# Eight row tiles normed one by one, six of them on GpSimd, and a last output unit in two banks with plain stores

## The chip, the cores and the metric

One core of a Trainium2 chip runs the whole kernel. Its engines work side by side, each through its own list in order: TensorE (PE; its weight loads are PEld), VectorE (DVE), ScalarE (ACT), GpSimd (POOL) and SyncE (SP), which issues most of the DMAs. They wait for one another by semaphores. The metric is device time in microseconds (us) of one execution, the median of several runs.

## The reference

The input x (called q) has 2048 rows of 1024. It is normed by rows, and two branches and x itself are summed:

```python
xn = _layernorm(x, axis=-1)                 # (x - mean) / sqrt(var + 1e-5)
return x + _A_ref(xn, k, v, shift_k, ssm_k, ssm_D) + _B_ref(xn, w1, w2)
# _A_ref: q * (long causal convolution of (short convolution of k) * v, by FFT over 4096 points)
# _B_ref: silu(xn @ w1) @ w2        w1: 1024 x 3584, w2: 3584 x 1024
```

## The kernel before

All matrix products run on TensorE in float16. Each operand is split into a high and a low float16 part, and three products stand for one in float32 (lines 979 to 984 and 1111 to 1117). The split of a factor is one instruction on ScalarE for the high part and one on VectorE for the low part (`split`, line 370). The first product of the feed-forward (x by w1) runs over pairs of 128 columns of w1; most pairs are computed in units of seven products of half-size blocks (`units`), the first two pairs directly (`plain_unit`). The second product (by w2) runs the same way, ends with eight such units of seven products (`units2`), and the last of these ends the kernel. The convolution's transforms run between these units on VectorE, ScalarE and TensorE.

The order is set by a planner (`Order.run`, line 167). Each stream of work is a generator that yields operations with an assumed duration; the planner takes the one that could start earliest, less the bias of its stream, and writes it down on its engine. What was written down is the program, and no engine changes its order later. While the constant stream is set (`order.spare`), the planner fills assumed gaps of TensorE with matmuls of constants that nothing reads.

The start goes like this. SyncE loads the 16 row tiles `xt` (128 rows by 1024 each) and the blocks of w1 (`x` and `raw`). For a tile VectorE takes two `bn_stats` and a `bn_aggr` (mean and variance into `stat`), GpSimd raises variance + 1e-5 to the power -0.5 (`rstd`), and the tile is normed in place (subtract the mean, multiply by `rstd`). Tiles 0 and 1 are treated alone, 2 and 3 together, 4 to 7 together, 8 to 15 together (`ln_rows`, line 528). Tiles 3, 5 and 7 are normed on ScalarE, with `nmr` = -mean * `rstd` as bias; the other five of the first eight on VectorE. TensorE transposes a normed tile in two halves into banks `ft` (three banks in turn; a fourth, `nm`, takes the small sums of squares of w1), and ScalarE and VectorE split them into the operands `x` (x_215 and x_216 for tiles 0 to 3). The first plain unit works through its rows in parts (tile 0, tile 1, tiles 2 and 3), and for each part through both column blocks j (`wo_190` and `wo_191`).

The last unit of `units2` (u = 7) has three result banks: `c` for P7 and P4, `two` for P6, P5 and P3, `one` for P1 and P2. P4 is added into `c` in two halves of 256 columns, and each half is scaled, summed and stored by a plain DMA from SyncE (line 1242). The other results go out by DMAs from GpSimd's queue that add to what is in memory (`G`).

## Time and profile before

| | us |
|---|---|
| median of 3 runs (lowest to highest) | 1247.47 (1245.33 to 1250.55) |
| the profiled execution | 1249.43 |
| its span, first to last instruction | 1247.7 |
| TensorE busy in it | 1230.0 |
| VectorE, ScalarE, GpSimd busy | 1120.0, 744.7, 142.6 |

TensorE's busy time counts a matmul until its modelled end, so a wait shows a little shorter than it is. A row of a timeline gives start, duration, engine, line, operation, what is written and read, a count where equal instructions are merged, and in brackets the idle time ahead of it with what ended it. Line numbers are those of the kernel before.

### The profile page before, as it was taken

What the parts mean: (1) busy time and instruction counts of PE and PEld (TensorE: products, weight loads), DVE (VectorE), ACT (ScalarE), POOL (GpSimd) and SP (SyncE); (2) the same over time, 40 slices, a digit from 0 to 9 for tenths busy, and PEclk for the clock granted to TensorE, in tenths of its full rate; (3) what the DMA queues carried; (4) which work ended last, traced back from release to release, by engine and by line L of the source; (5) the groups of instructions that cost most, each with busy time, mean ns of one, the idle gap of its engine ahead of it and who ended that gap; (6) DMA issues with size and microseconds to landing.
All of it is one profiled execution on the core that took longest, in us unless ns stands there. A gap on an engine that the chain in (4) does not pass through costs nothing.

```text
span 1247.7 us, 17185 instructions
## 1 busy us (share of the span) xinstructions
PE 1230.0 (99%) x6089; PEld 593.7 (48%) x6089; DVE 1120.0 (90%) x1360; ACT 744.7 (60%) x1303; POOL 142.6 (11%) x155
## 2 busy tenths in 40 slices
PE   8999999999999999999999999999999999999998
PEld 6544544444444444445444444544454454445444
DVE  7999996988799879998999799889979979998992
ACT  7867987878677767758663632563273264526231
POOL 1100000000000020002010300310030030113114
PEclk9999999999999999999999999999999999999999
DMA  9268998989999798969998787699596587978766
GB/s 337 77 223 301 329 311 274 301 277 350 302 357 287 252 260 269 277 213 266 338 293 228 154 264 177 153 250 269 126 214 172 134 169 239 252 157 139 164 144 93
DMA packets 254293, 292.93 MB, mean 235 GB/s; under 512 B 48768, under 2 KB 167808, under 8 KB 252032
## 3 DMA queue, kind: packets, MB, share of 16 engines
q1 hardware_dynamic: 227472, 266.93, 68.2%
q0 software_dynamic: 26736, 24.92, 14.9%
q8 instruction: 47, 0.77, 0.2%
q14 instruction: 38, 0.31, 0.1%
HBM read 193.22 MB, written 98.57 MB: 234 GB/s over the span
## 4 chain that ended last, share of the span: by engine, by line
PE 70%; DVE 18%; DMA 5%; issue 3%; ACT 2%; POOL 0%; SPq 0%; DVEq 0%; ACTq 0%
PE ff L981 10%; PE ff L982 10%; PE ff L983 10%; PE ff L1114 10%; PE ff L1116 10%; PE ff L1115 10%; DVE spec L349 6%; DVE tmp L349 2%; PE ps L1581 2%; PE ps L1583 2%; PE ps L1582 2%; DVE x L352 2%; DVE ht L352 1%; DMA wraw<-in_w 1%; DVE hf L349 1%
## 5 line engine op out<-in xcount | busy, mean ns | idle before, releaser
L1114 PE MATMUL ff<-x,wo 128*128 128x512 f16 x868 | 328.1, 378 | 1.8 <-ACT hf L360 1.2
L1116 PE MATMUL ff<-x,wo 128*128 128x512 f16 x868 | 328.1, 378 | 0.0
L1115 PE MATMUL ff<-x,wo 128*128 128x512 f16 x868 | 328.1, 378 | 0.0
L981 PE MATMUL ff<-x,wo 128*128 128x512 f16 (+2 forms) x824 | 304.1, 371 | 1.6 <-ACT wo L360 1.4
L983 PE MATMUL ff<-x,wo 128*128 128x512 f16 (+2 forms) x824 | 304.1, 371 | 1.5 <-DVE wo L352 1.4
L982 PE MATMUL ff<-x,wo 128*128 128x512 f16 (+2 forms) x824 | 304.1, 371 | 0.7 <-DVE x L352 0.7
L349 DVE TENSOR_TENSOR spec<-spec 128x1024 f32<-128x1024 f32 (+2 forms) x272 | 263.3, 1001 | 2.3
L1114 PEld LDWEIGHTS <-wo 128*128 128x128 f16 x868 | 84.9, 98 | 101.8 <-issue 1.3
L1116 PEld LDWEIGHTS <-wo 128*128 128x128 f16 x868 | 84.9, 98 | 101.6
L1115 PEld LDWEIGHTS <-wo 128*128 128x128 f16 x868 | 84.9, 98 | 101.6 <-issue 2.2
L983 PEld LDWEIGHTS <-wo 128*128 128x128 f16 x824 | 80.6, 98 | 94.7 <-DVE wo L352 1.8
L981 PEld LDWEIGHTS <-wo 128*128 128x128 f16 x824 | 80.6, 98 | 90.1 <-ACT wo L360 1.6
L982 PEld LDWEIGHTS <-wo 128*128 128x128 f16 x824 | 80.5, 98 | 87.3 <-issue 0.5
L346 POOL DMA_DIRECT2D out<-hf x59 | 52.0, 884 | 452.2 <-ACT hf L360 335.9
L360 ACT ACTIVATE hf<-ff,invc 128x512 f32<-128x512 f32 x60 | 40.9, 681 | 100.2 <-PE ff L1116 74.8
L346 POOL DMA_DIRECT2D out<-yt x56 | 62.3, 1300 | 335.1 <-DVE yt L352 195.2
L349 DVE TENSOR_TENSOR tmp<-spec 128x2048 f32<-128x2048 f32 (+1 forms) x48 | 92.6, 1934 | 0.9
L352 DVE SCALAR_TENSOR_TENSOR ht<-hf,wsc,ht 128x1024 f16<-128x1024 f32 (+1 forms) x56 | 67.2, 1203 | 12.8 <-ACT ht L360 12.7
L360 ACT ACTIVATE spec<-spec 128x1024 bf16<-128x1024 f32 x32 | 33.7, 1054 | 62.3 <-DVE spec L349 62.2
L360 ACT ACTIVATE spec<-ps 128x512 f32<-128x512 f32 x96 | 55.5, 591 | 18.8 <-PE ps L1583 17.2
L352 DVE SCALAR_TENSOR_TENSOR wo<-raw,wsc,wo 128x512 f16<-128x512 f32 (+1 forms) x56 | 56.6, 1013 | 10.0 <-ACT wo L360 9.5
L360 ACT ACTIVATE ht<-hf,wsc 128x1024 f16<-128x1024 f32 (+1 forms) x56 | 60.6, 1085 | 4.4 <-DVE hf L349 2.8
(175 smaller groups left out, 1759.8 us busy)
## 6 DMA issues: line engine op xcount, KB each, us to landing
wo<-hs SPq DMA_DIRECT2D x160, 256.0 KB, 3.7
hs<-ht SPq DMA_DIRECT2D x80, 256.0 KB, 4.8
wraw<-in_w SPq DMA_DIRECT2D x31, 512.0 KB, 5.4
out<-hf POOLq DMA_DIRECT2D x59, 256.0 KB, 4.2
raw<-in_w SPq DMA_DIRECT2D x28, 512.0 KB, 6.3
kin<-in_kp SPq DMA_DIRECT2D x16, 704.0 KB, 6.1
kf<-in_fs SPq DMA_DIRECT2D x8, 1024.0 KB, 5.5
hsfS<-ht SPq DMA_DIRECT2D x32, 256.0 KB, 3.8
```

Of the source, the lines that this page charges most:

```text
L346: return Op("POOL", 1.1, 4.8, lambda: nc.gpsimd.dma_start(o, i, accum_op=ADD), [i], [o], m, n)
L349: return V(lambda: nc.vector.tensor_tensor(o, a, b, op=op), o, [a, b], **k)
L352: return V(lambda: nc.vector.scalar_tensor_tensor(o, a, s, b, op0=op0, op1=op1), o, [a, b] + ([] if isinstance(s, float) else [s]), **k)
L360: nc.scalar.activation(o, i, func, scale=scale, **kw)
L981: nc.tensor.matmul(o, w[:, 0, k], xf[:, :, k, 0], start=first and k == 0, stop=False, **kw)
L982: nc.tensor.matmul(o, w[:, 0, k], xf[:, :, k, 1], start=False, stop=False, **kw)
L983: nc.tensor.matmul(o, w[:, 1, k], xf[:, :, k, 0], start=False, stop=last and k == KH - 1, **kw)
L1114: nc.tensor.matmul(o, hx[:, n, 0, :], wc[:, n, 0, q], start=first and n == 0, stop=False, **kw)
L1115: nc.tensor.matmul(o, hx[:, n, 0, :], wc[:, n, 1, q], start=False, stop=False, **kw)
L1116: nc.tensor.matmul(o, hx[:, n, 1, :], wc[:, n, 0, q], start=False, stop=last and n == 3, **kw)
L1581: nc.tensor.matmul(o, cf[:, 0], hi[i], start=i == 0, stop=False, **kw)
L1582: nc.tensor.matmul(o, cf[:, 0], lo[i], start=False, stop=False, **kw)
```

## The change

In the start, `ln_rows` makes a stream for each of tiles 0 to 7 (`norm_rows`), and each tile has its own chain on GpSimd: -mean, variance + 1e-5, the power, `nmr`. Tiles 2 to 7 are normed on GpSimd too; tiles 0 and 1 stay on VectorE, and ScalarE norms none. The scratch tiles `st` and `mv` get six buffers in place of two. The constant matmuls at the very start are 18 in place of 26. The banks `ft` and `nm` become one ring of four, in which late transposes leave one free. In the first plain unit both parts of the first two tiles run for column block 0 before block 1. The planner assumes the first DMAs to land 1 us earlier.

In the last unit, P7 and P4 go to two banks, one for columns 0 to 383 and one for 384 to 511. The tile that P3 ends (`at(u, 0, 1)`) is no longer added to memory from GpSimd's queue: its present value is loaded ahead of time (`o2`), summed on VectorE and stored by a plain DMA.

```diff
@@ -179,7 +179,8 @@
             _, t, s = best
             op, (r, w) = s.head, s.touched
             if self.spare is not None and op.eng == "PE":
-                for _ in range(int((t - self.free["PE"] - 0.1) / 0.22)):
+                op.fills = max(0, int((t - self.free["PE"] - 0.1) / 0.22))
+                for _ in range(op.fills):
...
@@ -191,7 +192,7 @@
             done = t + op.busy
             end = done + op.late
             if op.nbytes:
-                self.pipe = max(self.pipe, t + 3.0) + op.nbytes / 330e3
+                self.pipe = max(self.pipe, t + (2.0 if t < 3.0 else 3.0)) + op.nbytes / 330e3
...
@@ -430,8 +431,7 @@
-    ft = Ring(order, ps_e, "ft", 3)
-    nm = Ring(order, ps_e, "nm", 1)
+    nm = ft = Ring(order, ps_e, "ft", 4)
...
     def ln_rows():
-        for t0, n, bias in ((0, 1, 0.26), (1, 1, 0.26), (2, 2, 0.17), (4, 4, 0.15), (8, 8, 0.03)):
-            yield bias
+        for t in range(8):
+            add(norm_rows(t, 1), (0.26, 0.26, 0.17, 0.17, 0.1, 0.1, 0.1, 0.1)[t])
+        for t in range(8):
+            yield flag["xn", t]
+        yield from norm_rows(8, 8)
+
+    def norm_rows(t0, n):
+            yield flag["xt", t0]
             q = slice(t0, t0 + n)
-            mv = lnp.tile([P, 8], F32, name="mv", bufs=2)
-            m = mv[:, 0:n]
+            mv = lnp.tile([P, 2, 8], F32, name="mv", bufs=6)
+            m, minus = mv[:, 0, 0:n], mv[:, 1, 0:n]
             order_in = (8, 9, 12, 13, 10, 11, 14, 15) if n == 8 else range(t0, t0 + n)
             for t in order_in:
                 yield flag["xt", t]
                 xt = xts[t][0]
-                st = lnp.tile([P, 2, 6], F32, name="st", bufs=2)
+                st = lnp.tile([P, 2, 6], F32, name="st", bufs=6)
                 for a in range(2):
                     yield V(lambda: nc.vector.bn_stats(st[:, a, :], xt[:, a * W:(a + 1) * W]), st[:, a, :],
                             [xt[:, a * W:(a + 1) * W]], us=0.65)
                 yield V(lambda: nc.vector.bn_aggr(stat[:, t, :], st), stat[:, t, :], [st], us=0.2)
 
             def chain(m=m, q=q):
+                if n < 8:
+                    nc.gpsimd.tensor_scalar(minus, stat[:, q, 0], -1.0, None, op0=MUL)
                 nc.gpsimd.tensor_scalar(m, stat[:, q, 1], 1e-5, None, op0=ADD)
                 nc.gpsimd.tensor_tensor(rstd[:, q], m, power, op=ALU.pow)
-                if n in (2, 4):
-                    nc.gpsimd.tensor_scalar(m, stat[:, q, 0], -1.0, None, op0=MUL)
-                    nc.gpsimd.tensor_tensor(nmr[:, q], m, rstd[:, q], op=MUL)
             power = half.to_broadcast([P, n])
-            p = V(chain, rstd[:, q], [stat[:, q, :]], us=1.2)
+            p = V(chain, rstd[:, q], [stat[:, q, :]], us=1.0 + 0.25 * n)
             p.eng = "POOL"
-            p.writes.append(m)
-            if n in (2, 4):
-                p.busy += 0.5
-                p.writes.append(nmr[:, q])
+            p.writes += [m, minus]
             yield p
+            if n < 8:
+                p = V(lambda: nc.gpsimd.tensor_tensor(nmr[:, q], minus, rstd[:, q], op=MUL), nmr[:, q],
+                      [minus, rstd[:, q]], us=0.3)
+                p.eng = "POOL"
+                yield p
             if n == 8:
                 yield V(lambda: nc.vector.scalar_tensor_tensor(nmr, stat[:, :, 0], -1.0, rstd, op0=MUL, op1=MUL),
                         nmr, [stat, rstd])
             for t in order_in:
                 xt = xts[t][0]
-                if t in (3, 5, 7):
+                if t in (2,3,4,5,6,7,):
+                    p = V(lambda: nc.gpsimd.tensor_scalar(xt, xt, stat[:, t, 0:1], rstd[:, t:t + 1], op0=SUB, op1=MUL),
+                          xt, [xt, stat[:, t, :], rstd[:, t:t + 1]], us=1.2)
+                    p.eng = "POOL"
+                    yield p
+                    flag["xn", t].set()
+                    continue
+                if t in ():
                     yield a_act(xt, xt, AF.Identity, rstd[:, t:t + 1], nmr[:, t:t + 1])
                     flag["xn", t].set()
                     continue
...
             yield flag["xn", t]
             xn, tok = xns[t]
-            yield ft.ready
+            yield ft.ready if t < 8 else lambda: len(ft.free()) > 1
             pt, ptok = ft.tile([P, KH, P], uses=2)
...
-        for q, j in [(slice(([0] + list(ends))[n], e), j) for n, e in enumerate(ends) for j in range(2)]:
+        parts_of_rows = [slice(([0] + list(ends))[n], e) for n, e in enumerate(ends)]
+        todo = [(q, j) for q in parts_of_rows for j in range(2)]
+        if len(ends) == 3:
+            todo = [(q, j) for j in range(2) for q in parts_of_rows[:2]] + todo[4:]
+        for q, j in todo:
...
             c = ff.tile([P, W])
-            add(evacuate2(u, one, c, made, seen), EB)
-            yield from product2("P7", u, c[0], True)
+            banks = [c]
+            if last:
+                banks.append(seen["more"])
+            add(evacuate2(u, one, banks, made, seen), EB)
+            for q, bank in zip(columns(u), banks):
+                if bank is not c:
+                    yield ff.ready
+                    bank.what = ff.tile([P, W])
+                    bank = bank.what
+                yield from product2("P7", u, bank[0], True, q=q)
...
             yield seen["P7"]
-            for q in columns(u):
-                yield from product2("P4", u, c[0], q=q)
+            for q, bank in zip(columns(u), banks):
+                yield from product2("P4", u, (c if bank is c else bank.what)[0], q=q)
                 made["P4", q.start].set()
 
     def columns(u):
 
-        m = 2 if u == len(tiles2) - 1 else 1
-        return [slice(a * W // m, (a + 1) * W // m) for a in range(m)]
+        if u < len(tiles2) - 1:
+            return [slice(0, W)]
+        return [slice(0, 384), slice(384, W)]
...
-    def evacuate2(u, one, c, made, seen):
...
@@ -1214,6 +1241,9 @@
             yield hfs.ready
             o, otok = hfs.tile([P, W])
             yield L(o, at(u, 1, 0))
+            yield hfs.ready
+            o2, otok2 = hfs.tile([P, W])
+            yield L(o2, at(u, 0, 1))
...
         seen["P5"].set()
-        yield v_stt(d, c[0], invc2[:, 0:1], d, MUL, ADD)
+        banks = [banks[0]] + [b.what for b in banks[1:]]
+        for q, c in zip(columns(u), banks):
+            yield v_stt(d[:, q], c[0][:, q], invc2[:, 0:1], d[:, q], MUL, ADD)
...
         yield made["P3"]
-        add(copied(two, k2, at(u, 0, 1)), EB)
-        for q in columns(u):
+        if last:
+            yield v_stt(o2, two, invc2[:, 0:1], o2, MUL, ADD)
+            k2.set()
+            yield L(at(u, 0, 1), o2)
+            otok2.set()
+        else:
+            add(copied(two, k2, at(u, 0, 1)), EB)
+        for q, c in zip(columns(u), banks):
             yield made["P4", q.start]
             yield v_stt(a[:, q], c[0][:, q], invc2[:, 0:1], a[:, q], MUL, ADD)
+            c[1].set()
             yield (L if last else G)(at(u, 1, 0)[:, q], a[:, q])
-        c[1].set()
...
         yield flag["spilled"]
-        yield nm.ready
+        yield lambda: len(ft.free()) == 4
...
         pt, tok = ff.tile([P, 4, P])
-        for _ in range(26):
+        for _ in range(18):
             yield T(lambda: nc.tensor.matmul(pt[:, 0, :], ones, ones, start=True, stop=True), pt[:, 0, :], [], 0.3)
```

GpSimd's list at the start before, for tiles 2 and 3 and then 4 to 7 (545 to 549 are the chain's lines; tiles 0 and 1 have the first two of them each):

```order
L545 TENSOR_SCALAR mv<-stat 128x2 [waits DVE_49]
L546 TENSOR_TENSOR rstd<-mv,half 128x2 [waits Pool_49]
L548 TENSOR_SCALAR mv<-stat 128x2 [waits Pool_49]
L549 TENSOR_TENSOR nmr<-mv,rstd 128x2 [waits Pool_49]
L545 TENSOR_SCALAR mv<-stat 128x4 [waits DVE_49]
L546 TENSOR_TENSOR rstd<-mv,half 128x4 [waits Pool_49]
L548 TENSOR_SCALAR mv<-stat 128x4 [waits Pool_49]
L549 TENSOR_TENSOR nmr<-mv,rstd 128x4 [waits Pool_49]
```

And now for tile 2, whose rows return for each of tiles 3 to 7 (L571 is the norm; tiles 0 and 1 have the first four):

```order
L552 TENSOR_SCALAR mv<-stat 128x1 [waits DVE_49]
L553 TENSOR_SCALAR mv<-stat 128x1
L554 TENSOR_TENSOR rstd<-mv,half 128x1 [waits Pool_49]
L561 TENSOR_TENSOR nmr<-mv,rstd 128x1 [waits Pool_49]
L571 TENSOR_SCALAR xt_242<-xt_242,stat,rstd 128x1024 [waits DMAHW0_49]
```

Each tile has four small instructions in place of two to four for a group, and a norm of 128x1024 stands in the same list between a tile's chain and the next one's.

VectorE's list, from the norm of tile 1 (xt_237) on; xt_242 and xt_246 are tiles 2 and 3, `ft_342` and `ft_365` the transposed halves of tile 1:

```order
L567 TENSOR_SCALAR xt_237<-xt_237,stat,rstd 128x1024 [waits Pool_49]
L352 SCALAR_TENSOR_TENSOR wo_190<-x_225,wsc,wo_190 128x512 [waits DMAHW3_49,DMAHW2_49,Activation_49]
L540 BN_STATS st<-xt_242 128x6 [waits DMAHW0_49]
L352 SCALAR_TENSOR_TENSOR wo_190<-x_225,wsc,wo_190 128x512 [waits DMAHW5_49,DMAHW4_49,Activation_49]
L352 SCALAR_TENSOR_TENSOR wo_191<-x_225,wsc,wo_191 128x512 [waits Activation_49]
L540 BN_STATS st<-xt_242 128x6
L542 BN_AGGR stat<-st 128x2 [waits DVE_49]
L540 BN_STATS st<-xt_246 128x6 [waits DMAHW1_49]
L352 SCALAR_TENSOR_TENSOR x_215<-ft_342,x_215 128x4x128 [waits PE_49,Activation_49]
L352 SCALAR_TENSOR_TENSOR x_216<-ft_365,x_216 128x4x128 [waits PE_49,Activation_49]
L540 BN_STATS st<-xt_246 128x6
L352 SCALAR_TENSOR_TENSOR wo_191<-x_225,wsc,wo_191 128x512 [waits Activation_49]
```

And now (xt_249 is tile 3, xt_264 tile 4, `ft_355` and `ft_379` the halves of tile 1):

```order
L581 TENSOR_SCALAR xt_237<-xt_237,stat,rstd 128x1024 [waits Pool_49]
L353 SCALAR_TENSOR_TENSOR wo_190<-x_224,wsc,wo_190 128x512 [waits DMAHW3_49,DMAHW2_49,Activation_49]
L546 BN_STATS st<-xt_242 128x6
L353 SCALAR_TENSOR_TENSOR wo_190<-x_224,wsc,wo_190 128x512 [waits DMAHW5_49,DMAHW4_49,Activation_49]
L548 BN_AGGR stat<-st 128x2 [waits DVE_49]
L546 BN_STATS st<-xt_249 128x6 [waits DMAHW1_49]
L546 BN_STATS st<-xt_249 128x6
L353 SCALAR_TENSOR_TENSOR x_215<-ft_355,x_215 128x4x128 [waits PE_49,Activation_49]
L353 SCALAR_TENSOR_TENSOR x_216<-ft_379,x_216 128x4x128 [waits PE_49,Activation_49]
L548 BN_AGGR stat<-st 128x2 [waits DVE_49]
L546 BN_STATS st<-xt_264 128x6 [waits DMAHW4_49]
L353 SCALAR_TENSOR_TENSOR wo_191<-x_224,wsc,wo_191 128x512 [waits Activation_49]
```

Tile 2's mean and variance come after two low parts of weights in place of three, both parts for `wo_191` stand behind the low parts of tile 1, and tile 3's `bn_stats` ahead of them.

The end of VectorE's list before, from the last output of the convolution on (`hf_196` is the loaded output, `ff_10328` the bank `c`):

```order
L352 SCALAR_TENSOR_TENSOR wo_195<-ps_10292,csc_8745,ht_199 128x512 [waits DMASW3_49,DMASW2_49,DVE_49]
L352 SCALAR_TENSOR_TENSOR hf_197<-ff_10328,invc_156,hf_197 128x512 [waits Activation_49]
L349 TENSOR_TENSOR hf_197<-hf_197,hf_196 128x512 [waits DMAHW6_49]
L352 SCALAR_TENSOR_TENSOR hf_197<-ff_10328,invc_156,hf_197 128x256 [waits DVE_49,PE_49]
L352 SCALAR_TENSOR_TENSOR hf_197<-ff_10328,invc_156,hf_197 128x256 [waits PE_49]
```

And now, from P7's two sums on (`ff_10352` and `ff_10372` are the two banks, `ff_10353` is `two`):

```order
L353 SCALAR_TENSOR_TENSOR hf_197<-ff_10352,invc_156,hf_197 128x384 [waits Activation_49]
L353 SCALAR_TENSOR_TENSOR hf_197<-ff_10372,invc_156,hf_197 128x128 [waits PE_49]
L350 TENSOR_TENSOR hf_197<-hf_197,hf_196 128x512 [waits DMAHW6_49]
L353 SCALAR_TENSOR_TENSOR hf_196<-ff_10353,invc_156,hf_196 128x512 [waits DMAHW7_49,PE_49]
L353 SCALAR_TENSOR_TENSOR hf_197<-ff_10352,invc_156,hf_197 128x384 [waits DVE_49,PE_49]
L353 SCALAR_TENSOR_TENSOR hf_197<-ff_10372,invc_156,hf_197 128x128 [waits PE_49]
```

P4's two sums at the end have 384 and 128 columns in place of twice 256, each with a bank of its own, and the sum for the plain store of `at(u, 0, 1)` is new ahead of them.

SyncE's last DMAs before:

```order
L337 DMA wo_191<-hsfS_71 128x1024 [waits DMAHW4_49,PE_49]
L337 DMA wo_190<-hsfA_72 128x1024 [waits DMAHW5_49,PE_49]
L337 DMA hf_196<-out 128x512 [waits DMAHW6_49,DMASW1_49,DVE_49]
L337 DMA out<-hf_197 128x256 [waits DMAHW7_49,DMAHW6_49,DVE_49]
L337 DMA out<-hf_197 128x256 [waits DMAHW0_49,DVE_49]
```

And now, from the load for the last unit on:

```order
L338 DMA hf_196<-out 128x512 [waits DMAHW6_49,DMASW1_49,DVE_49]
L338 DMA hf_196<-out 128x512 [waits DMASW6_49,DMAHW7_49,DMASW5_49,DMASW3_49]
L338 DMA out<-hf_196 128x512 [waits DMAHW7_49,DMAHW0_49,DVE_49]
L338 DMA out<-hf_197 128x384 [waits DMAHW6_49,DMAHW1_49,DVE_49]
L338 DMA out<-hf_197 128x128 [waits DMAHW2_49,DVE_49]
```

One load and one store of 128x512 are new on SyncE's queue, and the last store has 128 columns in place of 256. GpSimd's last DMA (`out<-wo_190`, of P3) is gone from its list, and with it ScalarE's last copy.

On TensorE 11 wide constant matmuls stand ahead of the first transposes in place of 5, and 16 in place of 15 ahead of those of tile 1; the sums of squares come between the two halves of tile 0. The two filler matmuls in the middle of the program are there in both, and one more has come ahead of the first unit of the lower rows.

1 line of the change is left out of this document (added).

## The prediction

> **What bounds the kernel now.** I read the page's busy line first, then the windows of TensorE over the whole span, then the timelines of its start and the chain at the end. The page says that TensorE is busy nearly throughout:
>
> ```profile
> span 1247.7 us, 17185 instructions
> PE 1230.0 (99%) x6089; PEld 593.7 (48%) x6089; DVE 1120.0 (90%) x1360; ACT 744.7 (60%) x1303; POOL 142.6 (11%) x155
> ```
>
> So 17.7 us are left in which TensorE does nothing. The windows of 25 us (TensorE's busy time and count, granted clock, DMA share, GB/s) show where they lie:
>
> ```profile
> 0.00:25.00 25.00, 21.08 (x200) 1.00 0.94 344
> 25.00:50.00 25.00, 22.36 (x148) 1.00 0.54 161
> 50.00:75.00 25.00, 25.00 (x120) 1.00 0.29 98
> 675.00:700.00 25.00, 21.45 (x101) 0.93 0.50 118
> 1225.00:1247.70 22.70, 17.36 (x92) 1.00 0.73 101
> ```
>
> There are 6.56 in the first 50 us, 3.55 in one stretch in the middle that the diff does not touch, and 5.34 at the end (a part of which is the last store). The change works at the first and the last place, so it can win some five of those ten microseconds, plus what it saves of constants, and no more; what it does in the start is kept only if TensorE stays full behind it. TensorE's timeline of the start:
>
> ```profile
> 1.06 7.96 PE L1844 MATMUL ff<-one 128*128 128x128 f32 x52 [1.06 <-DVE oneb L403]
> 8.86 1.25 PE L1847 MATMUL ff<-oneb 128*128 128x512 bf16 x5
> 9.95 1.04 PE L586 MATMUL ft<-ident,xt 128*128 128x128 f32 x8
> 10.95 3.44 PE L1847 MATMUL ff<-oneb 128*128 128x512 bf16 x15
> 14.26 1.09 PE L586 MATMUL ft<-ident,xt 128*128 128x128 f32 x8
> 15.19 0.22 PE L981 MATMUL ff<-x,wo 128*128 128x128 f16 x1
> 15.24 0.22 PE L982 MATMUL ff<-x,wo 128*128 128x128 f16 x1
> 18.98 0.23 PE L981 MATMUL ff<-x,wo 128*128 128x128 f16 x1 [1.41 <-ACT wo L360]
> 20.68 0.23 PE L983 MATMUL ff<-x,wo 128*128 128x128 f16 x1 [1.41 <-DVE wo L352]
> 26.91 0.66 PE L586 MATMUL ft<-ident,xt 128*128 128x128 f32 x4 [1.43 <-ACT xt L360]
> 29.70 0.27 PE L982 MATMUL ff<-x,wo 128*128 128x256 f16 x1 [0.72 <-DVE x L352]
> ```
>
> The first 15 us hold constants, then come four waits that sum to 4.97: two for split weights, one for a normed tile that ScalarE finishes (L360), one for a low part on VectorE. The windows leave 6.56 - 1.06 - 4.97 = 0.53 for some six small ones. A shown wait is shorter than the true one: fifteen wide constants take 3.44 and five 1.25, so one costs 0.219 and each group ends in a tail of 0.15 that counts as busy. Ten waits are thus 5.5 + 1.5 = 7.0 us.
>
> **The constants.** 26 matmuls in float32 are 52 passes; 18 are 36. The passes at the end of the row are the fast ones: 52 in 7.96 less the slower first ones. The row up to the 45th pass is
>
> ```profile
> 1.06 7.18 PE L1844 MATMUL ff<-one 128*128 128x128 f32 x45 [1.06 <-DVE oneb L403]
> ```
>
> so one costs 0.78/7 = 0.11, and sixteen fewer give back 1.8. Six more wide constants (11 for 5) cost 6 x 0.219 = 1.3. The transposes of tile 0 come at about 9.5 instead of 9.95. VectorE's low parts of tile 0 follow them, and then the norm of tile 1, on which tile 1's transposes at 14.26 hang. In the new order one `bn_stats` stands between, so I keep 0.4 of the 0.5: first real matmul at 14.8, **-0.4**. Bounds: 0 (if tile 1's norm does not move) and -0.5.
>
> **The norms.** GpSimd's, VectorE's and ScalarE's rows for the chains and norms (group of two for tiles 2 and 3; then four):
>
> ```profile
> 0.24 0.10 POOL L1906 MEMSET const-float32-0.0<- 128x1 f32 x1 [0.24 <-issue]
> 1.00 0.29 POOL masks.py:199 TENSOR_SCALAR_AFFINE_SELECT ident<-ident 128x128 f32<-128x128 f32 x1
> 11.03 0.58 POOL L546 TENSOR_TENSOR rstd<-mv,half 128x1 f32<-128x1 f32 x1
> 20.83 0.23 POOL L545 TENSOR_SCALAR mv<-stat 128x2 f32<-128x2 f32 x1 [9.23 <-DVE stat L542]
> 21.95 0.80 POOL L548 TENSOR_SCALAR mv<-stat 128x2 f32<-128x2 f32 x1
> 17.42 0.21 DVE L542 BATCH_NORM_AGGREGATE stat<-st 128x2 f32<-128x12 f32 x1
> 21.90 0.81 DVE L567 TENSOR_SCALAR xt<-xt,stat,rstd 128x1024 f32<-128x1024 f32 x1 [0.36 <-POOL rstd L546]
> 33.38 1.53 DVE L567 TENSOR_SCALAR xt<-xt,stat,rstd 128x1024 f32<-128x1024 f32 x2 [0.94 <-POOL rstd L546]
> 23.06 1.24 ACT L360 ACTIVATE xt<-xt,nmr,rstd 128x1024 f32<-128x1024 f32 x1 [1.01 <-POOL nmr L549]
> 35.00 2.38 ACT L360 ACTIVATE xt<-xt,nmr,rstd 128x1024 f32<-128x1024 f32 x2 [2.79 <-POOL nmr L549]
> ```
>
> Before, tile 2's variance is ready at 17.63, but the chain waits for tile 3 and starts at 20.83; tile 2 is normed at 22.71, tile 3 at 24.30, tiles 4 and 6 at 34.91, 5 and 7 at 37.38. VectorE sheds three norms (3 x 0.8 = 2.4), ScalarE three (3 x 1.24 = 3.7). GpSimd gets 32 small instructions in place of 12, and six norms, all in series.
>
> A tile's chain on GpSimd is 0.23 for the first instruction, 0.1 more for the second like it, 0.58 for the power, 0.23 for `nmr` and some 0.1 between them: 1.2 us. What a norm of 128x1024 costs there no row shows. From below: 0.81, VectorE's time; the select of 128x128 gives nearly the same, if the 0.23 of an instruction of two columns is its fixed part: 0.23 + 8 x 0.06 = 0.7. From above: if only 0.10 of the select is fixed, as much as a memset of one column takes, 0.10 + 8 x 0.19 = 1.6; if none is, 8 x 0.29 = 2.3. Between 0.8 and 1.6, which have a fixed part, I take the middle, 1.2, since no row is nearer, and keep 0.8 and 2.3 as ends.
>
> GpSimd and VectorE also stand in each other's way. L548 takes 0.80 at 21.95 where its like L545 takes 0.23, and it ends within 0.04 of VectorE's norm that started at 21.90. L545 for four tiles does the same beside two low parts of weights (0.62, to 31.87; the first of the two low parts ends at 31.08 + 1.36/2 = 31.76):
>
> ```profile
> 31.25 0.62 POOL L545 TENSOR_SCALAR mv<-stat 128x4 f32<-128x4 f32 x1 [8.23 <-DVE stat L542]
> 31.08 1.36 DVE L352 SCALAR_TENSOR_TENSOR wo<-x,wsc,wo 128x512 f16<-128x512 f32 x2
> ```
>
> So one small instruction of a chain in the way of such a VectorE instruction loses up to 0.7, and a GpSimd norm holds VectorE's low parts of weights for up to 1.2. The Trainium skill (SBUF — State Buffer, Who interferes with whom) says that a VectorE instruction with two SBUF inputs or in a two-port mode and a GpSimd instruction exclude each other for a whole instruction; the 0.80 beside the 0.81 agrees.
>
> With these durations in the new order I get: tile 2's variance after norm 1 (which ends 0.4 earlier), one low part of 0.7, a `bn_stats`, another low part and 0.21, at 15.8; plus chain 1.2 and norm 1.2 and gaps, 18.5 (was 22.7). Tile 3's variance is now behind the two low parts of tile 1, at 18.4; its chain loses 0.6 to a low part; normed 21.6 (24.3). Tiles 4 and 5 follow at 24.8 and 27.8 (34.2 and 36.2, half way through the rows of two). Tiles 6 and 7 lose: their `bn_stats` stand far down VectorE's list behind eight low parts, so 38.2 and 42.4 (34.9 and 37.4).
>
> What TensorE then waits for: 1.3 up to 17.7 (tile 0's 24 matmuls for column block 0 end 24 x 0.055 after 14.8, at 16.1, and tile 1's need its first low part, which VectorE ends at 17.7 behind two `bn_stats` of tile 3; this takes the place of both waits for weights, since column block 1 comes later), 1.0 at 21.7 (tile 3), 0.5 at 23 (a bank of the ring that VectorE frees), 1.3 at 42.5 (tile 7), and 0.8 of small ones: 4.9 in place of 7.0, **-2.1**. One more filler on TensorE, **+0.2**. The DMAs of the start are the same ones in the same order on SyncE; nothing is moved there. The ring of four leaves late transposes one bank fewer; the window from 50 on, with TensorE 25.00 of 25.00 busy, hides that.
>
> How it hangs on the norm's duration: up to 1.3 nothing is lost (tile 3 alone waits). At 1.6 the wait at tile 3 is 0.4 longer, tiles 4, 5 and 7 a bit later: about -2.5 in all for the whole change. At 2.0 five norms in series are 4 us later than at 1.2, most of it hidden except at tiles 3 and 7, and the sum is about -0.5; the break-even lies near 2.0. From there every norm of the series shows: 0.3 more in five of them is 1.5, and VectorE's low parts, held as long, cost about another 1, so at 2.3 it is +2.
>
> **The end.** TensorE's and VectorE's last rows, in one list by time:
>
> ```profile
> 1236.46 0.75 DVE L352 SCALAR_TENSOR_TENSOR hf<-ff,invc,hf 128x512 f32<-128x512 f32 x1 [8.38 <-ACT hf L360]
> 1241.28 0.27 PE L1116 MATMUL ff<-x,wo 128*128 128x256 f16 x1
> 1241.59 0.48 DVE L352 SCALAR_TENSOR_TENSOR hf<-ff,invc,hf 128x256 f32<-128x256 f32 x1 [3.78 <-PE ff L1116]
> 1242.12 0.27 PE L1114 MATMUL ff<-x,wo 128*128 128x256 f16 x1 [0.57 <-DVE hf L352]
> 1242.98 0.48 DVE L352 SCALAR_TENSOR_TENSOR hf<-ff,invc,hf 128x256 f32<-128x256 f32 x1 [0.91 <-PE ff L1116]
> ```
>
> TensorE stops in P4 until VectorE has read the first half, since both halves stand in one bank: the matmul of 1242.12 would have come at 1241.39, 0.11 after the one before it. With two banks this 0.73 is gone. P4 does not get longer by its new columns: 128-column matmuls follow one another by 0.055 (15.19, 15.24), half of 0.11. VectorE's sum of 384 columns, 0.61 between 0.48 and 0.75, lies beside the twelve matmuls of the second bank (12 x 0.055 = 0.66) and just ends in time. The last sum has 128 columns; by the line through 0.75 and 0.48 it takes 0.34, so -0.14. Then the store, and GpSimd's last adding DMAs of the convolution:
>
> ```profile
> 1229.35 2.20 POOL L346 DMA_DIRECT2D out<-wo  x2 [0.30 <-DMA out<-wo]
> hf<-out SPq DMA_DIRECT2D x1, 256.0 KB, 4.0
> out<-hf SPq DMA_DIRECT2D x2, 128.0 KB, 3.4
> ```
>
> The last plain store is half as large, and P3's adding DMA no longer runs beside it, so -0.2 of 3.4 (between 0 and -0.6). Together **-1.1**, bounds -0.5 and -1.5. The added sum of P3 (0.75 on VectorE) lies under the first 384 columns of P4, twelve matmuls of some 0.16 each, 1.9. The added load waits for the convolution's last adding DMAs, issued by GpSimd up to 1231.55; the last starts about 1230.4, and if it takes about as long as the load (4.0) it lands about 1234.5. Another 4.0 for the load is 1238.5, and it is needed when P3 ends, about 1239.7 (P4's 18 matmuls to 1241.39 begin 18 x 0.11 earlier). If that cover of some 1.2 us fails, VectorE's list stops there, P4's sums stand behind it, and each microsecond late is one more in the end.
>
> **The sum.** -0.4 - 2.1 + 0.2 - 1.1 = -3.4 to -3.5. The profiled execution took 1249.43, 1.96 above the median, so it would be 1245.9, and the median **1244.0**.
>
> **The rivals.** (a) GpSimd's norm is short (0.8, the select's row with 0.23 fixed) and the lock costs nothing: tile 3's wait of 1.0, half of tile 7's and the small rest at the bank go, 2.0 in all: 1242.0. (b) It is 1.6, the same row with 0.10 fixed, or twice VectorE's 0.81: -2.0 to -2.5, so 1245.3. The Trainium skill (GPSIMD Engine Reference, Performance versus the Vector engine) has GpSimd about twice as slow in elementwise work, 4497 ns against 2293; by it the estimate would be 1245.3 as well, and no run here shows it yet. (c) The other side: the norm costs 2.3, the whole select scaled. From 2.0 on the norms in series are what TensorE waits for (tiles 3, 4, 5 and 7): +2.1, 1249.6. For it speaks only that nothing is known of the fixed part; against it, that even a memset of one column has 0.10. (d) The start's gain is given back: behind 50 us TensorE waits for nothing, but VectorE is just as full:
>
> ```profile
> 50.00:55.00 5.00, 5.00 (x25) 2.25 (x23) 5.00 (x9) 4.97 (x9) 0.00 (x0) 1.00 0.14 57
> ```
>
> (TensorE, its loads, VectorE, ScalarE, GpSimd, then clock and DMA.) If the operands made there are on the edge, TensorE comes earlier and waits the same; only the end's -1.1 stays: 1246.4. Against it: VectorE sheds 2.4 and ScalarE 3.7 before that.
>
> **The chances.** Main case 0.44, (a) 0.16, (b) 0.14, (c) 0.13, (d) 0.13. The main case's own range is 1242 to 1246, by the bounds of the start, the end and the middle of the norm's. The whole range, 1240.0 to 1249.5, takes in (a) with the largest end gain and most of (c). A measurement of this kernel can tell about 0.5% from no change, 6.2 us here. Faster than 1241.2 asks for (a) and every bound on the good side: 0.12. Slower than 1253.7 asks for a norm of some 3 us or the late load at the end: 0.04. Within: 0.84.
>
> **What would show it.** In the profile after: the norm's row on GpSimd between 1.0 and 1.4; first real matmul at 14.8; normed tiles 2 and 3 at 18.5 and 21.6, 6 and 7 later than before; waits of TensorE at about 17.7, 21.7 and 42.5, in sum 1.5 to 2 less than before in the first 50 us; from 50 to 75 still 25.00 busy; no wait between the halves of P4 and a last sum of about 0.33. A norm over 2 us, a new wait between 50 and 100, or a wait of VectorE for the loaded tile at 1239 would make it wrong.

## The result, and the profile after

| us | before | after |
|---|---|---|
| median (lowest to highest) | 1247.47 (1245.33 to 1250.55) | 1255.77 (1253.95 to 1258.54) |
| profiled execution, and its span | 1249.43, 1247.7 | 1258.54, 1256.8 |
| TensorE busy | 1230.0 | 1234.0 |

The changed kernel is slower by 0.6%: its time over that before is 1.0063, with a 95% interval of 1.0044 to 1.0081. That is 8.3 us by the medians, and 9.1 between the profiled executions; the one after is the slowest of its five.

The page after, the line of busy times:

```profile
PE 1234.0 (98%) x6094; PEld 596.6 (47%) x6094; DVE 1119.0 (89%) x1359; ACT 741.8 (59%) x1299; POOL 167.5 (13%) x180
```

GpSimd is busy 25 us more, for six norms and some small instructions. TensorE's windows after (busy time and count, granted clock, DMA share, GB/s), the first three stretches, the one that answers to 675 to 700 before (the changed kernel is some 9 us later there), and one further on:

```profile
0.00:25.00 25.00, 19.53 (x155) 0.95 0.94 341
25.00:50.00 25.00, 20.30 (x148) 0.84 0.44 134
50.00:75.00 25.00, 22.48 (x113) 1.00 0.22 62
...
684.00:709.00 25.00, 23.78 (x124) 1.00 0.53 147
...
1075.00:1100.00 25.00, 22.06 (x100) 0.96 0.91 233
```

TensorE idles 12.7 us of the first 75, where before it idled 6.6, and it also runs at a lower clock. GpSimd's timeline after says why; here are all rows of tile 2's chain and norm, then the norms of tiles 3 to 7:

```profile
16.22 0.23 POOL L552 TENSOR_SCALAR mv<-stat 128x1 f32<-128x1 f32 x1 [3.71 <-DVE stat L548]
16.51 0.21 POOL L553 TENSOR_SCALAR mv<-stat 128x1 f32<-128x1 f32 x1
16.80 0.57 POOL L554 TENSOR_TENSOR rstd<-mv,half 128x1 f32<-128x1 f32 x1
17.45 0.19 POOL L561 TENSOR_TENSOR nmr<-mv,rstd 128x1 f32<-128x1 f32 x1
17.62 3.81 POOL L571 TENSOR_SCALAR xt<-xt,stat,rstd 128x1024 f32<-128x1024 f32 x1
...
23.10 3.80 POOL L571 TENSOR_SCALAR xt<-xt,stat,rstd 128x1024 f32<-128x1024 f32 x1
...
28.39 3.80 POOL L571 TENSOR_SCALAR xt<-xt,stat,rstd 128x1024 f32<-128x1024 f32 x1
...
34.46 3.80 POOL L571 TENSOR_SCALAR xt<-xt,stat,rstd 128x1024 f32<-128x1024 f32 x1
...
44.92 3.80 POOL L571 TENSOR_SCALAR xt<-xt,stat,rstd 128x1024 f32<-128x1024 f32 x1
...
50.48 3.80 POOL L571 TENSOR_SCALAR xt<-xt,stat,rstd 128x1024 f32<-128x1024 f32 x1
```

A norm takes 3.80, against 0.81 on VectorE and 1.24 on ScalarE, and with its chain a tile takes 5.2 to 6.0 in one list. Tile 2 is done at 21.4 (22.7 before), tile 3 at 26.9 (24.3), tile 4 at 32.2 (34.2), tile 5 at 38.3 (36.2), tile 6 at 48.7 (34.9), tile 7 at 54.3 (37.4). Only tiles 2 and 4 gain. TensorE's timeline shows all its waits of the start:

```profile
17.92 0.22 PE L996 MATMUL ff<-x,wo 128*128 128x128 f16 x1 [1.07 <-DVE x L353]
21.48 1.09 PE L600 MATMUL ft<-ident,xt 128*128 128x128 f32 x8 [2.12 <-POOL xt L571]
26.96 1.12 PE L600 MATMUL ft<-ident,xt 128*128 128x128 f32 x4 [3.18 <-POOL xt L571]
38.31 1.09 PE L600 MATMUL ft<-ident,xt 128*128 128x128 f32 x8 [2.21 <-POOL xt L571]
48.78 1.09 PE L600 MATMUL ft<-ident,xt 128*128 128x128 f32 x8 [0.53 <-POOL xt L571]
54.34 1.09 PE L600 MATMUL ft<-ident,xt 128*128 128x128 f32 x8 [2.52 <-POOL xt L571]
```

Five waits for a GpSimd norm sum to 10.56 us. Behind the first of them, from 22.7 to 32.9 us, the granted clock is halved (all engines by windows of 2 us; the clock is the third figure from the right):

```profile
22.00:24.00 2.00, 1.77 (x21) 1.50 (x19) 0.22 (x1) 1.83 (x4) 1.84 (x4) 0.67 1.03 412
24.00:26.00 2.00, 0.00 (x0) 0.00 (x0) 1.89 (x5) 0.24 (x1) 2.00 (x1) 0.50 1.05 365
...
30.00:32.00 2.00, 2.00 (x21) 2.00 (x20) 2.00 (x5) 2.00 (x6) 2.00 (x1) 0.50 0.31 103
32.00:34.00 2.00, 2.00 (x20) 1.89 (x18) 2.00 (x4) 1.94 (x4) 1.77 (x4) 0.77 0.08 19
```

The order written for TensorE is the same before and after from about 250 us on, up to the last unit, so a landmark in it measures the lag. Four matmuls of zeros stand in both; first before, then after:

```profile
320.33 0.61 PE L332 MATMUL ff<-one,zero 128*128 128x128 f32 x4
```

```profile
329.59 0.61 PE L333 MATMUL ff<-one,zero 128*128 128x128 f32 x4
```

The lag is 9.26 us there. Of it 6.1 are idle time (12.7 less 6.6). The other 3.2 are the same work taking longer, which fits the clock: of the 10.2 us at half TensorE waits 3.2, and in the other 7.0 it does the work of 3.5. The end is 9.1 late. In between the lag falls and rises again: the stretch from 675 lost 3.55 before and the one from 684 loses 1.22 after, but near 1098 after waits longer than before. First after, then before, each time a wait that ScalarE ends:

```profile
1098.77 0.58 PE L1132 MATMUL ff<-x,wo 128*128 128x512 f16 x1 [2.94 <-ACT hf L361]
```

```profile
1091.21 0.38 PE L1114 MATMUL ff<-x,wo 128*128 128x512 f16 x1 [1.20 <-ACT hf L360]
```

Whether that exchange belongs to the change is one of the questions below.

The end came out nearly as read before. VectorE's last two rows after:

```profile
1249.71 0.75 DVE L353 SCALAR_TENSOR_TENSOR hf<-ff,invc,hf 128x512 f32<-128x512 f32 x1 [1.69 <-PE ff L1134]
1251.66 1.02 DVE L353 SCALAR_TENSOR_TENSOR hf<-ff,invc,hf 128x384 f32<-128x384 f32 x2 [1.20 <-PE ff L1134]
```

The sum of P3 waits for TensorE, not for its load; the last two sums follow one another without a gap, and no wait of TensorE within P4 is left.

### The profile page after: what moved, and what is told of

Same layout as the page of the kernel before. It is cut to its first block, busy times and chain, and to the rows that moved or that the text cites. A ratio compares the mean times of both kernels' runs of the same rounds, so it can differ in the third digit from the quotient of the medians.

```text
span 1256.8 us, 17232 instructions
## 1 busy us (share of the span) xinstructions
PE 1234.0 (98%) x6094; PEld 596.6 (47%) x6094; DVE 1119.0 (89%) x1359; ACT 741.8 (59%) x1299; POOL 167.5 (13%) x180
## 4 chain that ended last, share of the span: by engine, by line
PE 72%; DVE 16%; DMA 5%; issue 3%; POOL 3%; ACT 1%; SPq 0%; DVEq 0%; ACTq 0%
PE ff L1132 12%; PE ff L1133 12%; PE ff L1134 12%; PE ff L995 10%; PE ff L996 10%; PE ff L997 10%; DVE spec L350 5%; DVE tmp L350 2%; POOL xt L571 2%; DMA out<-yt 2%; DVE ht L353 2%; PE ps L1619 2%; PE ps L1621 2%; PE ps L1620 2%; DVE x L353 1%
## 5 line engine op out<-in xcount | busy, mean ns | idle before, releaser
L1132 PE MATMUL ff<-x,wo 128*128 128x512 f16 (+2 forms) x872 | 329.6, 378 | 2.9 <-ACT hf L361 2.9
L1133 PE MATMUL ff<-x,wo 128*128 128x512 f16 (+2 forms) x872 | 329.7, 378 | 0.0
L1134 PE MATMUL ff<-x,wo 128*128 128x512 f16 (+2 forms) x872 | 329.4, 378 | 0.0
L996 PE MATMUL ff<-x,wo 128*128 128x512 f16 (+2 forms) x824 | 306.1, 372 | 1.1 <-DVE x L353 1.1
L997 PE MATMUL ff<-x,wo 128*128 128x512 f16 (+2 forms) x824 | 306.1, 372 | 0.0
L995 PE MATMUL ff<-x,wo 128*128 128x512 f16 (+2 forms) x824 | 306.0, 372 | 0.0
```

The source lines that it names most:

```text
L995: nc.tensor.matmul(o, w[:, 0, k], xf[:, :, k, 0], start=first and k == 0, stop=False, **kw)
L996: nc.tensor.matmul(o, w[:, 0, k], xf[:, :, k, 1], start=False, stop=False, **kw)
L997: nc.tensor.matmul(o, w[:, 1, k], xf[:, :, k, 0], start=False, stop=last and k == KH - 1, **kw)
L1132: nc.tensor.matmul(o, hx[:, n, 0, :], wc[:, n, 0, q], start=first and n == 0, stop=False, **kw)
L1133: nc.tensor.matmul(o, hx[:, n, 0, :], wc[:, n, 1, q], start=False, stop=False, **kw)
L1134: nc.tensor.matmul(o, hx[:, n, 1, :], wc[:, n, 0, q], start=False, stop=last and n == 3, **kw)
```

## The experiments

Theory G was at first that GpSimd's norms are the whole loss; rival H that the chains by tile, the ring of four and the order of the blocks cost as well.

### The norms put back, the end alone, the start alone

```diff
-                if t in (2,3,4,5,6,7,):
+                if t in ():
...
-                if t in ():
+                if t in (3, 5, 7):
```

> The changed kernel with one edit: tiles 2, 4 and 6 are normed on VectorE and 3, 5 and 7 on ScalarE, as before the change; the chains by tile, the ring, the order of the blocks and the end stay. Theory G (GpSimd's norm of 3.80 us, six times in one list, is the whole loss): the five waits of TensorE for a GpSimd norm (10.56 us) and the halved clock behind them go, and what the prediction saw for the rest stays: TensorE 2 to 4 us ahead of the kernel before at 75 us, no wait above 1.5 in the start, median 1243 to 1246. Rival H (the chains by tile, the ring of four and the new order of blocks cost as well): waits of 2 us or more remain in the first 50 us, and the median is 1249 or more.

Measured: median 1254.97, ratio to before 1.006 (1.0045 to 1.0075). By the time alone theory G would be dead: no norm is left on GpSimd, and nearly nothing is won. The trace says otherwise. In the first 75 us TensorE is busy 70.91 (68.45 before, 62.32 in the changed kernel), and no wait there exceeds 1.09. The loss is further on (TensorE's timeline, then all engines in the 5 us around the first of these waits):

```profile
518.69 1.16 PE L333 MATMUL ff<-one,zero 128*128 128x128 f32 x8 [2.22 <-DVE hf L350]
...
586.61 1.16 PE L333 MATMUL ff<-one,zero 128*128 128x128 f32 x8 [1.90 <-ACT hf L361]
...
786.23 0.38 PE L1619 MATMUL ps<-hl,cfw 128*128 128x512 f16 x1 [2.47 <-ACT tmp L361]
```

```profile
515.00:520.00 5.00, 2.78 (x17) 1.67 (x16) 4.96 (x7) 3.60 (x6) 0.00 (x0) 1.00 0.61 161
```

VectorE is full (4.96 of 5, the third figure after the window's length) while TensorE waits for it, at places where neither other kernel waits as long. The edit changed durations that the planner assumes, so it wrote another program: the four matmuls of zeros near 320 us aren't there, and eight in a row stand at 518 and at 586. So this run changes two things at once, and what it tells of the norms is only its start.

```diff
+ units2, columns and evacuate2 of the changed kernel in the kernel before
```

> The kernel before with the last unit of the changed kernel alone. By the trace of the changed kernel the wait within P4 is gone and 4.7 us lie between the last matmul and the end of the span instead of 5.0. Theory G: nothing else moves, -0.9 (0.65 + 0.27), median about 1246.6, start and middle as before. Rival: the added load, store and sum cost elsewhere at the end, no gain or a loss: 1247.5 or more.

Measured: median 1247.28, ratio 0.9995 (0.9984 to 1.0006). In its trace the wait within P4 is gone. But from the start of the last matmul to the end of the span it takes 5.24, against 5.00 before and 4.69 in the changed kernel, so the 0.3 that the smaller last store was to give isn't steady. A gain of 0.9 is inside the interval as is none: inconclusive for the time.

```diff
+ units2, columns and evacuate2 of the kernel before in the changed kernel
```

> The changed kernel with the last unit of the kernel before. Theory G: the start carries the whole loss, so it is 0.9 slower than the changed kernel: 1256.7, and 9 to 10 us behind the kernel before at 75 us. Rival: part of the loss comes from the end, and this is faster than the changed kernel: below 1255.

Measured: median 1257.76, ratio 1.0082 (1.0069 to 1.0095). The start carries the whole loss; this is 2.0 over the changed kernel by the medians, of which the end's 0.9 was expected.

### What GpSimd asks for 1024 columns

```diff
+                if n == 8:
...
+                    nc.gpsimd.memset(s0, 1.0)
+                    for k in (1024, 512, 128):
+                        nc.gpsimd.tensor_scalar(s0[:, :k], s0[:, :k], s1, s2, op0=SUB, op1=MUL)
+                    nc.gpsimd.tensor_scalar(s0, s0, s1, None, op0=MUL)
+                    nc.gpsimd.tensor_scalar(s0, s0, 0.5, 0.25, op0=SUB, op1=MUL)
+                    nc.gpsimd.tensor_scalar(s0, s0, 0.5, None, op0=MUL)
+                    nc.gpsimd.tensor_tensor(s0, s0, s0, op=MUL)
+                    nc.gpsimd.tensor_copy(s0, s0)
```

> The kernel before with nine more instructions on GpSimd, on a scratch tile that nothing else reads, behind the chain of tiles 8 to 15, where GpSimd's list is empty for long: a memset of 1024 columns; the norm's form (two operations, each with a scalar per row) at 1024, 512 and 128 columns; one operation with a scalar per row, two with constants, one with a constant, a product of two tensors and a copy, all at 1024. In the changed kernel the norm takes 3.80. If its time goes by the element (3.7 ns), 512 columns take 1.9 to 2.0 and 128 some 0.5 to 0.6; if a fixed part is large, 512 takes clearly more than half. If the scalars per row are dear, the two operations with constants take 1.5 us or less; if each operation counts, one takes half of two; if GpSimd is slow with any 1024 columns, all forms take 3 us or more. The select of 128x128 in the start (0.29, or 1.5 ns for each element beyond a fixed 0.10) speaks for large differences between forms.

GpSimd's timeline (`s0` is the scratch tile, `s1` and `s2` hold a scalar per row; the first row, L554, holds three sizes, which take 4090 ns for 1024 columns, 2386 for 512 and 1137 for 128):

```profile
101.53 7.82 POOL L554 TENSOR_SCALAR scr<-scr,stat 128x1024 f32<-128x1024 f32 x3
109.44 3.81 POOL L555 TENSOR_SCALAR scr<-scr,stat 128x1024 f32<-128x1024 f32 x1
113.33 3.95 POOL L556 TENSOR_SCALAR scr<-scr 128x1024 f32<-128x1024 f32 x1
117.37 2.95 POOL L557 TENSOR_SCALAR scr<-scr 128x1024 f32<-128x1024 f32 x1
120.40 2.40 POOL L558 TENSOR_TENSOR scr<-scr 128x1024 f32<-128x1024 f32 x1
122.87 1.92 POOL L559 COPY scr<-scr 128x1024 f32<-128x1024 f32 x1
```

The form decides: 1.92 for a copy, 2.40 for a product of two tensors, 2.95 to 3.95 for a tensor with scalars. One operation with a scalar per row costs as much as the norm's two (3.81), and so do two with constants (3.95): neither the scalars per row alone nor the second operation alone explains the price. None is below 1.9, so none of these forms would have met the 1.2 that I took. Each was run once, beside VectorE's work, which draws some of them out (L554's 4.09 is the norm that takes 3.80 elsewhere). The sizes show that the time goes mostly by the element: 1.70 us for 512 columns more, 1.25 for 384 more. What is left for a fixed part can't be told from what VectorE draws out.

### The same order, other engines

To change the engine and nothing else, the planner must go on booking the norms on GpSimd:

```diff
-                    p = V(lambda: nc.gpsimd.tensor_scalar(xt, xt, ...
+                    def norm(xt=xt, t=t):
+                        if t in ():
+                            nc.gpsimd.tensor_scalar(xt, xt, ...
+                        elif t in (3, 5, 7):
+                            nc.scalar.activation(xt, xt, AF.Identity, scale=rstd[:, t:t + 1], bias=nmr[:, t:t + 1])
+                        else:
+                            nc.vector.tensor_scalar(xt, xt, stat[:, t, 0:1], rstd[:, t:t + 1], op0=SUB, op1=MUL)
+                    p = V(norm, xt, ...
```

> The changed kernel's written order, kept word for word on all engines, with one edit: the six norms are issued at the same places of the order, but by VectorE (tiles 2, 4, 6) and ScalarE (3, 5, 7) instead of GpSimd; the planner still books them on GpSimd. In the run with the norms put back and planned anew the start was 3.4 us ahead of the kernel before and the end 2 behind in the profiled execution, with new waits of TensorE near 516, 584 and 783 us where its list of matmuls differs from both other kernels; the changed kernel and the kernel before have the same list from some 200 us on up to the last unit. Theory P (GpSimd's 3.80 us are the whole loss of the changed kernel; what the run with a new plan lost, its plan lost): no new wait in the middle, TensorE level with the kernel before at 75 us or up to 2 us ahead, median 1244.5 to 1247.5. Rival H (chains by tile, ring and blocks cost as well): behind the kernel before at 75 us by 3 us or more, median 1251 or more.

Measured: median 1245.66, ratio to before 0.9981 (0.9971 to 0.9991): 10.1 below the changed kernel, and 9.3 below the run planned anew with the norms on the same engines. The landmark and the start:

```profile
320.42 0.61 PE L333 MATMUL ff<-one,zero 128*128 128x128 f32 x4
...
25.00:50.00 25.00, 23.42 (x176) 1.00 0.61 192
50.00:75.00 25.00, 25.00 (x120) 1.00 0.27 92
```

TensorE's list is that of the changed kernel, matmul for matmul. It is 0.09 behind the kernel before at the landmark, the clock stays at 1.00, and the middle has no long new wait (one of 0.89 near 903, where the run of the end alone, with the list of the kernel before, has 1.29). Theory P holds: in this order GpSimd's norms are the loss of the changed kernel, by their waits and the half clock behind them, and the new plan is the loss of the first experiment. Rival H falls: chains, ring and blocks together cost nothing that shows, and with the norms off GpSimd the change gains 1.9.

### Two norms on GpSimd

```diff
-                        if t in ():
+                        if t in (2, 3):
...
-                        elif t in (3, 5, 7):
+                        elif t in (5, 7):
```

> As the run with the changed kernel's order kept, but tiles 2 and 3 are normed by GpSimd, 4 and 6 by VectorE, 5 and 7 by ScalarE. In the changed kernel TensorE waits 2.12 and 3.18 us for these two norms and 5.26 for tiles 5, 6 and 7 (4 is in time). Theory P: the two norms carry their share, 3.5 to 5 us over the run with none on GpSimd, so 1248 to 1251.5, and 4 to 6 below the changed kernel. Rival: the loss comes only when all six stand in series, and two cost under 1.5 us.

Measured: median 1248.85, ratio 1.0009 (0.9998 to 1.002). The landmark stands here:

```profile
323.82 0.61 PE L333 MATMUL ff<-one,zero 128*128 128x128 f32 x4
```

That is 3.40 behind the run with none on GpSimd, and 3.2 by the medians: a little under the 3.5 expected, but not the rival's 1.5. Two of the six norms carry a third of the 10.1; TensorE waits 2.13 and 3.10 for them, as in the changed kernel. In the first 75 us it idles 7.6, only 1.6 more than in the run with none on GpSimd, and its first real matmul comes 0.58 earlier. So 2.4 of the lag is the same work taking longer, at a clock of 0.93 in these 75 us instead of 1.00.

### Is a late start kept to the end?

The kernel before in its own order, with 42 more constants in the emission of the 26th:

```diff
-        for _ in range(26):
-            yield T(lambda: nc.tensor.matmul(pt[:, 0, :], ones, ones, start=True, stop=True), ...
+        for k in range(26):
+            yield T(lambda k=k: [nc.tensor.matmul(pt[:, 0, :], ones, ones, start=True, stop=True)
+                                 for _ in range(43 if k == 25 else 1)], ...
```

> The kernel before in its own order with 42 more constant matmuls behind the first 26, 42 x 2 passes x 0.112 = 9.4 us, about the changed kernel's lag at 75 us (9.3). Theory K (a lag of the start is kept to the end, the middle gives nothing back): 9.4 slower than before, median 1256.9, TensorE's waits of the start as long as before. Rival M (the wait near 691 us and those behind it take up part of a late start; in the changed kernel's profile the lag fell from 8.9 to 5.0 there): 1251 to 1254.

Measured: median 1257.54, ratio 1.0067 (1.0049 to 1.0084). By the medians that is 10.0 for 9.4 put in, so nothing shows of a lag given back, though the interval, 6.1 to 10.5 us, touches the upper end of rival M. In the profile the lag changes on the way, in the same order as before: the end is 9.4 late, the landmark 11.36. TensorE's waits of the middle are others. The one near 691 is 0.74, where the kernel before has 2.54; the one of 1.20 that ends at 1091.21 before isn't there, but some 12 us ahead of its place in the list stands one that the kernel before doesn't have:

```profile
1089.77 0.38 PE L1114 MATMUL ff<-x,wo 128*128 128x512 f16 x1 [1.76 <-ACT ff L360]
```

So the waits near 691 and 1090 have another length in each execution: 2.5 and 1.2 before, 1.2 and 2.9 after, 1.5 and 1.4 in the run with the same order and the norms moved, 2.4 and 1.0 in the run of the start alone, whose start is the changed kernel's. What the middle gave and took in the changed kernel's profile goes with the execution, not with the change. Rival M finds no support.

The landmark is 2.0 later than the constants make it, and the clock accounts for most of that. The constants at the very start follow one another by 0.21 us at first and by 0.11 later; the pace changes at 5.06 us in the profile before and at 6.90 in this one. Some eight passes are 0.1 longer each, and the first real matmul is 10.20 late instead of 9.4. Behind it this execution has a stretch at a lower clock, 0.93 where the kernel before had 1.00:

```profile
25.00:50.00 25.00, 19.95 (x199) 0.93 0.32 101
```

### Other plans of the same work

The norms put back and planned anew once more, but with ScalarE taking tiles 2, 4 and 6:

```diff
-                if t in (3, 5, 7):
+                if t in (2, 4, 6):
```

> As the run with the norms put back and planned anew, but with ScalarE norming tiles 2, 4 and 6 and VectorE 3, 5 and 7. The work is the same; the planner makes another list from it. Theory P: the start is as short (3 to 5 us ahead of the kernel before at 75 us), and what follows depends on the list: if the waits of the kernel before near 691 and 1090 come back in place of those near 516, 584 and 783, the median is 1241 to 1244.5, some 11 below the run planned anew before. Rival: the loss of that run belongs to the work on VectorE and ScalarE, which is the same here, and the median is again 1252 or more.

Measured: median 1243.86, ratio 0.9961 (0.9943 to 0.998), 11.1 below the same edit with 3, 5 and 7. At 75 us TensorE has been busy 71.55, nearly as in that run (70.91); the waits near 516 and 783 are gone. By the median it is the fastest version here, ahead of both kernels; the next run lies within its interval, and the run with the same order and the norms moved overlaps it.

With the order of the blocks set back as well:

```diff
-        if len(ends) == 3:
-            todo = [(q, j) for j in range(2) for q in parts_of_rows[:2]] + todo[4:]
```

> As the run with another plan (ScalarE norms tiles 2, 4 and 6, VectorE 3, 5 and 7), with the order of the blocks of the first plain unit as before the change: both column blocks for each part of the rows. Theory P (the start is worth 3 to 5 us once no norm stands on GpSimd; the rest is the list that the planner makes): two waits for weights of 1.5 to 1.8 us come back near 18 and 20, and the wait for a norm near 25 goes, so the start is as long; the middle is a new list, and in place of waits near 691 and 1090 it may have others; median 1236 to 1245. Rival: the new order of the blocks is what made the start short; then 2 to 3 us over the run with another plan, 1246 or more.

Measured: median 1245.08, ratio 0.9967 (0.9954 to 0.9979); the two waits for weights are back with 1.47 and 1.29, the waits for tile 1's low part and for a norm are gone, and TensorE is busy 71.12 in the first 75 us. That is 0.08 over theory P's range and below the rival's 1246. The blocks' order makes no difference that can be told from the plan's. A further split of the norms (ScalarE 2, 5 and 6, planned anew; expected at 1238 to 1245) took 1248.88, ratio 1.001 (0.9999 to 1.0022). Its output is 0.048 from the reference for a reason that I did not find, so nothing is built on its time.

### A planner that knows the price

```diff
-                          xt, [xt, stat[:, t, :], rstd[:, t:t + 1]], us=1.2)
+                          xt, [xt, stat[:, t, :], rstd[:, t:t + 1]], us=3.8)
```

> The changed kernel with the planner's assumption for a norm on GpSimd raised from 1.2 to the 3.8 us that the chip takes; the norms stay on GpSimd. Theory P (the instruction itself is too slow in this place): the planner lays other work and constants into the waits, but five norms in series still take 19 us, and the start is as late as in the changed kernel or later: 9 to 15 us behind the kernel before at 75 us, median 1254 to 1262. Rival A (the loss comes from the planner's false price, not from the norm): with the true price the work in between fills the waits, and the median falls below 1250.

Measured: median 1255.45, ratio 1.0065 (1.0046 to 1.0085), as slow as the changed kernel. The expectation of 9 to 15 us behind at 75 us was too much. TensorE is busy 66.41 of the first 75 us there, 4 more than in the changed kernel and 2 fewer than before. A part of this is matmuls of zeros (22, busy 2.62, against 2 in the changed kernel); its matmuls on `wo`, the real work, are busy 44.96, against 49.48 before and 41.88 in the changed kernel, where some run at half the clock. So the true price wins back a part of the start, and some 4.5 us stay lost. This plan loses more further on, with a wait of 2.36 near 593 that the other two kernels don't have. Rival A's median is not met, but this run is a new program as well, and a new plan can move the median by 11 us. What it shows is the start: with the true price the norm is still too slow there, while a share of the changed kernel's loss, which this run can't measure, may be the planner's false price.

## Why the prediction was wrong

**The norm's price.** The step that failed is "Between 0.8 and 1.6, which have a fixed part, I take the middle, 1.2, since no row is nearer, and keep 0.8 and 2.3 as ends". The norm takes 3.80, 1.7 times the upper end; to a norm of some 3 us the prediction gave 0.04. The ends were made from VectorE's time and one row of GpSimd, a select of 128x128, scaled by the element. That row is another instruction on another form, and the prices run shows that forms of the same size differ by a factor of two on this engine; a bound from a different form bounds nothing. The upper end should have stayed open, since GpSimd's timeline before held no instruction wider than 128 columns.

**What follows from the price** held. The break-even near 2.0 and rival (c), norms in series that TensorE waits for at tiles 3, 5 and 7, are what happened, with tiles 2 and 6 in addition and tile 4 not; its chance of 0.13 and its 1249.6 hung on the same 2.3. The rival's own slope, 2.5 us for 0.3 from the break-even, would give some 14 over the kernel before at 3.8, where 8.3 were measured. Of the 2.5, 1 stood for low parts of VectorE that a norm holds, and the trace shows none held (see the lock below); without it the slope gives 8.5. That this is so near is luck in part: it counts five norms in full, where tile 4's costs TensorE nothing, and it has no term for the half clock, behind which some 3 of the lag in the profile lie.

**The rule of the Trainium skill** (GPSIMD Engine Reference, Performance versus the Vector engine: about twice VectorE's time, from a two-input sum) gave an estimate of 1.6. The measured norm is 4.7 times VectorE's 0.81. For the product of two tensors, the nearest to that sum, the prices run has 2.40 for 1024 columns, in line with the 4497 ns that the Trainium skill gives for 2048 in the same section. That number holds for its form and not for the norm's.

**The chains** take 1.4, not 1.2: in `16.22` and `16.51` the second instruction starts 0.29 after the first, where I let it overlap.

**The lock** was half right. Small instructions of a chain are drawn out beside VectorE's low parts of weights (in the changed kernel 0.59 instead of 0.21 at 32.58, 0.94 instead of 0.57 at 33.25). But I said that a GpSimd norm holds such a low part for up to 1.2, and it doesn't: VectorE's low part at 19.06, inside the norm from 17.62 to 21.43, takes

```profile
19.06 0.73 DVE L353 SCALAR_TENSOR_TENSOR wo<-x,wsc,wo 128x512 f16<-128x512 f32 x1
```

as long as the low part at 33.02, outside a norm (0.74), and that norm takes 3.81 where its likes take 3.80.

**The start's other terms.** The first real matmul came at 15.14 instead of 14.8, 0.05 earlier than before. That moves with the place at which the constants change from 0.21 us apart to 0.11: 5.06 before, 5.66 after. In the run with the norms put back it is 5.06 as before, and the first real matmul comes at 14.89, 0.30 earlier: so the -0.4 was nearly right, and the execution hid it. The wait for tile 1's low part (1.07 at 17.9) was forecast as 1.3 at 17.7. That the waits for weights go was right, and with the norms off GpSimd the start in the changed kernel's order is level with the one before, not 2 us ahead; planned for, TensorE has been busy 2.5 to 3.1 us more by 75 us (70.91 and 71.55 against 68.45).

**The end.** The wait within P4 went as worked out. The rest, 0.27 in the changed kernel's profile, isn't steady between executions, and the run of the end alone can't confirm 0.9 in all, where 1.1 was forecast.

**Rival (d)**, the start's lead given back behind 50 us, wasn't put to the test by the changed kernel, which has no lead. The two plans that are 3.1 and 2.7 ahead in busy time at 75 us (ScalarE norms 2, 4 and 6; with either order of the blocks) keep TensorE 25.00 of 25.00 busy from 50 to 75 and end 3.7 and 3.2 ahead. The plan of the first experiment is 2.5 ahead there and ends 7.4 behind, by waits from 516 us on, so a lead of the start isn't safe where the list behind it is new.

**The middle** that the diff does not touch was rightly left out of the sum, by its mean. But I had not thought of the planner as a term: where its assumptions change, all that follows may move, by 11 us between two plans of the same work.

## What to carry to other kernels

A price for an operation on an engine that has never run it at that size is unknown until it is run: keep its upper end open, and ask first how many times it stands in series. Where a planner writes the whole program from assumed durations, an edit in the start is a new program; test a part of a change with the written order held fixed, or the plan's luck (here 11 us) hides the part (here 10 us) altogether.
